# Block products for the second halves of the first two chunks of an attention-and-MLP kernel

## The chip, the cores and the metric

The kernel runs on one core of a Trainium2 chip. The core has a matrix engine (TensorE, PE in the profile), a vector engine (VectorE, DVE), a scalar engine (ScalarE, ACT), a general engine (GpSimd, POOL) and a sync engine (SyncE, SP) that issues most of the DMAs. The metric is the device time of one execution in microseconds (us).

## What is computed

Two blocks follow each other. The first is an attention whose feature map is a product of two small sketches; the second is an MLP with an exact GELU over all 4352 tokens:

```python
# q, k, v: (4 batches, 4 heads, 1088 tokens, 32); S1, S2: (8, 32)
def phi(x):
    a = np.einsum('rd,bhsd->bhsr', S1, x)
    b = np.einsum('rd,bhsd->bhsr', S2, x)
    return np.einsum('bhsi,bhsj->bhsij', a, b).reshape(*x.shape[:-1], 64)
q_p, k_p = phi(q), phi(k)
kv  = np.einsum('bhsf,bhsd->bhfd', k_p, v)
z   = np.sum(k_p, axis=2)
num = np.einsum('bhsf,bhfd->bhsd', q_p, kv)
den = np.einsum('bhsf,bhf->bhs', q_p, z)[..., None] + 1e-06
x   = (num / den).transpose(0, 2, 1, 3).reshape(4352, 128)
h   = x @ w_in                       # w_in (128, 2048)
g   = 0.5 * h * (1.0 + erf(h / sqrt(2)))
out = g @ w_out                      # w_out (2048, 128)
```

The weights arrive with 64 bits a number and are rounded to 32 bits on the chip.

## The kernel before

The tokens are worked in eight chunks of 512 (two for each batch) and a ninth of 256, which holds what is left of the four batches. For a chunk `n` the MLP runs over 16 inner tiles `fi` of 128 channels. A *step* is one pair `(n, fi)`. In a step TensorE makes the hidden product of the pair, ScalarE its GELU; the second half (the product with `w_out`) of an earlier pair, and pieces of attention for later chunks, are put into the same step.

The first hidden product and the GELU:

```python
def hidden(n, fi, by_halves=False):
    ps = hidden_bank()                              # one of two PSUM banks
    w = w_tile(w_in_sb, fi)
    for rows in (slice(0, 64), slice(64, 128)) if by_halves else (slice(0, 128),):
        pe.matmul(ps[rows, :W], lhsT=w[:, rows], rhs=xT[n][:, :W], start=True, stop=True)
    ...                                             # g_of[n, fi]: a tile "g", or a quarter of a "block"
    act.activation(out=g_of[n, fi][:, :W], in_=ps[:, :W], func=ACT.Gelu)
```

There are two ways for the second half. The usual one, for chunks 0, 1 and the last, adds 16 products in one PSUM bank:

```python
def project(n, fi, parts=range(B // 2)):
    first, final = fi == 0, fi == NF - 1
    if first:
        o_of[n] = out_bank() if n < NMAIN else [work_bank() for i in range(B // 2)]
    ...
    pe.matmul(o_of[n], lhsT=w_tile(w_out_sb, fi), rhs=g, start=first, stop=final)
```

The other, for chunks 2 to 7, splits pairs of tiles into 2x2 blocks and makes seven block products where there would be eight. Four sums of the weights are made once (`channel_sums`, GpSimd), four sums of the GELU's output for each block of four tiles (`token_sums`, GpSimd), and at the chunk's end the two PSUM banks are put together (`drain`, ScalarE and VectorE, and `combine`, VectorE):

```python
def token_sums(n, b):                               # after the GELU of tiles 4b to 4b + 3
    ...
    pool.tensor_sub(out=s[3], in0=a11, in1=a21)
    pool.tensor_add(out=s[1], in0=a21, in1=a22)
    pool.tensor_sub(out=s[2], in0=s[1], in1=a11)
    pool.tensor_sub(out=s[4], in0=a12, in1=s[2])

def two_products(n, b, i):                          # one of seven pairs of a block of four tiles
    ...
    if b == 0 and i == 0:
        acc[n] = [out_bank(), out_bank()]           # there are two out banks in all
    ...
        pe.matmul(acc[n][bank][half * 64:(half + 1) * 64, col:col + HW], lhsT=fixed, rhs=moving, ...)

def drain(n):
    act.copy(out=C[lo, 0], in_=a1[hi])
    act.copy(out=N[hi, 0, one], in_=a1[hi, one])
    act.copy(out=N[lo, 0, one], in_=a0[lo, one])
    dve.tensor_add(out=C[lo, 1], in0=a1[lo], in1=C[lo, 0])
    for half in (lo, hi):
        dve.tensor_add(out=C[half, 0, one], in0=a0[lo, one], in1=C[lo, 1, two])
    dve.tensor_add(out=C[hi, 0, two], in0=a0[hi, two], in1=C[hi, 0, one])
    dve.tensor_add(out=N[hi, 1, one], in0=a0[hi, one], in1=C[hi, 0, two])
    dve.tensor_add(out=N[lo, 1, one], in0=a0[lo, two], in1=N[lo, 0, one])
```

The order of the steps, and what is put into them (`at(step, what)`), for chunks 0 to 2:

```python
steps = [(n, fi) for f in range(0, NF, 4) for n in range(2) for fi in range(f, f + 4)]
steps += [(n, fi) for n in range(2, NCHUNK) for fi in range(NF)]
...
def round_at(t, w):                                 # from 64 bits to 32; takes a "bits_r" buffer, of which there are two
    at(t, lambda: (r.append(Rounding(w)), r[0].low_words(), r[0].fields()))
    at(t + 1, lambda: (r[0].exponents(), r[0].finish()))
for i, (t0, t1) in enumerate(((4, 6), (8, 10), (12, 20))):
    round_at(t0, w_in_sb[i + 2])
    round_at(t1, w_out_sb[i + 2])
for i in range(len(pieces)):
    at(22 + i, channel_sums, i)
b, t = 1, NCH * NF                                  # t = 32
at(t - 20, widen_v_rem, b)
for r in range(2):
    at(t - 18, key_turn_blocks, b, r)
for r in range(2):
    at(t - 17, features, b, r)
    at(t - 17, add_tokens, b, r, pool)              # writes k_s, in a "bits_r" buffer
at(t - 16, turn_keys_rem, b)
at(t - 15, features_rem, b)
at(t - 13, finish_keys, b)                          # TensorE reads k_s (L395); ScalarE copies kv_T
at(t - 12, lambda: turn_kv(1, held["kv"], by_act))
at(t - 13, query_turn, 2)
at(t - 11, query_expand, 2)
at(t - 8, attend, 2)
for n in range(3, NCHUNK):
    t = (n - 1) * NF
    at(t + 1 if n > 3 else t - 3, query_turn, n)    # VectorE, L452
    at(t + 2 if n > 3 else t - 2, query_expand, n)  # TensorE L461, ScalarE L468, VectorE L482
    ...
    at(t + 5, attend, n, ...)                       # TensorE L503, ScalarE L510, VectorE L511 and L515
```

`attend` ends in a chain: four copies on ScalarE, a reciprocal and four multiplies on VectorE, which make `xT[n]`. Within a step the text has this order: drains, the hidden product, token sums, the slots above, stores, second halves. Each engine works its instructions in the order of the text.

Of the kernel before, what the change touches and what calls it, by code (L numbers as in the profile page):

```python
# [16 lines left out]
def kernel(  # L17
# [33 lines left out]
    C = D + 1  # L51
    LAG = 2
    NMAIN = B * NCH
    FAST = 2
    NB = 4
    NCHUNK = NMAIN + 1
    assert B == 4 and d_model == 128 == H * D == JC * D == 2 * F and H == 4 and REM == 64 and NCH == 2

# [94 lines left out]

        return (a, 1) if a.dtype == FP else (a.bitcast(U32), 2)

    def load_w_in(i, gated=False):
        src, e = words(moe_w_in)
        c0, c1 = pieces[i]
        to = landing(w_in_sb[i], e == 2)
        if gated:  # L160

            pool.memset(to[0:1, 0:1], 0)
        sp.dma_start(out=to, in_=src[:, c0 * e:c1 * e])

    def load_w_out(i):
        src, e = words(moe_w_out)
        sp.dma_start(
            out=landing(w_out_sb[i], e == 2).rearrange("p (fo d) -> p fo d", d=d_model * e),
            in_=src[slice(*pieces[i]), :].rearrange("(fo fi) d -> fi fo d", fi=128))

    S_dst = landing(SR, S1.dtype != FP)
# [14 lines left out]
    load_q(1)  # L186
    load_w_in(1)
    load_w_out(0)
    load_w_out(1)

    def load_rest():

        for i in range(2, len(pieces)):
            load_w_in(i, gated=i == 2)
            load_w_out(i)
        for b in range(1, B):
            load_turned_k(b)
            load_main(sp, "v", b)
            for c in range(NCH):
                load_q(b * NCH + c)  # L200
            if b == 1:
                for n, b1 in (("k", 1), ("k", 3), ("v", 1), ("v", 2), ("v", 3)):
                    load_rem(n, b1)
        for b in range(B):
            load_rem("q", b)
# [224 lines left out]
        copy(out=kv_T[b], in_=ps[:, :128])  # L430

    def turn_kv(b, ps, copy):
        if b < 2:
            pe.transpose(ps[:, :128], in_=kv_T[b], identity=ident)
        else:
            for rows in (slice(0, 64), slice(64, 128)):
                pe.matmul(ps[rows, :128], lhsT=kv_T[b][:, rows], rhs=ident, start=True, stop=True)
        copy(out=kz[b].rearrange("p c n -> p (c n)"), in_=ps[:, :128])
# [119 lines left out]
    def hidden(n, fi, by_halves=False):  # L558
        W = width[n]
        ps = hidden_bank()  # L560
        w = w_tile(w_in_sb, fi)
        for rows in (slice(0, 64), slice(64, 128)) if by_halves else (slice(0, 128),):
            pe.matmul(ps[rows, :W], lhsT=w[:, rows], rhs=xT[n][:, :W], start=True, stop=True)  # L563
        if n < FAST:
            g_of[n, fi] = mlp.tile([128, CW], FP, name="g", bufs=4)
        else:
            if fi % NB == 0:
                blocks[n, fi // NB] = block(FP)
            g_of[n, fi] = blocks[n, fi // NB][:, fi % NB]
        act.activation(out=g_of[n, fi][:, :W], in_=ps[:, :W], func=ACT.Gelu)  # L570
# [40 lines left out]
    def factor(n, b, name, e):  # L611
# [9 lines left out]
        j = {"5": 1, "6": 2, "7": 3}[name[0]]  # L621
        return sums[n, b][j][:, e], T[j][:, k]

    def two_products(n, b, i):

        fours, ones_, sixes = [("4", "7", e, e) for e in range(2)], [("1", "5", e, e) for e in range(2)], ("6a", "6b", 0, 1)

        order = fours + ([sixes] + ones_ if b == 0 else ones_ + [sixes]) + [("2", "3", e, e) for e in range(2)]
        two = order[i]
        if b == 0 and i == 0:  # L630
            acc[n] = [out_bank(), out_bank()]
        for name, e in zip(two[:2], two[2:]):
            half, bank, col = PLACE[name]
            moving, fixed = factor(n, b, name, e)

            pe.matmul(acc[n][bank][half * 64:(half + 1) * 64, col:col + HW], lhsT=fixed, rhs=moving,  # L636
                      start=b == 0 and e == 0 and name in "4715", stop=b == NF // NB - 1, skip_group_check=True)

    drained = {}

    def drain(n):
# [15 lines left out]
        dve.tensor_add(out=N[lo, 1, one], in0=a0[lo, two], in1=N[lo, 0, one])  # L657
        drained[n] = C, N

    def combine(n):  # L660

        C, N = drained.pop(n)
        lo, hi, one, two = slice(0, 64), slice(64, 128), slice(0, HW), slice(HW, CW)
        dve.tensor_add(out=N[lo, 1, two], in0=C[lo, 1, one], in1=C[lo, 0, one])
        dve.tensor_add(out=N[hi, 1, two], in0=N[hi, 0, one], in1=C[hi, 0, two])
        return N[:, 1]

    def project(n, fi, parts=range(B // 2)):
        first, final = fi == 0, fi == NF - 1
        if first:  # L670
            o_of[n] = out_bank() if n < NMAIN else [work_bank() for i in range(B // 2)]
        g = g_of[n, fi]
        if n == NMAIN:

            for i in parts:
                pe.matmul(o_of[n][i][:, :128], lhsT=g[:, i * 128:(i + 1) * 128], rhs=w_tile(w_out_sb, fi),  # L676
                          start=first, stop=final)
            return
        pe.matmul(o_of[n], lhsT=w_tile(w_out_sb, fi), rhs=g, start=first, stop=final)  # L679

    def store(n):
        oT = mlp.tile([128, JC, d_model], FP, name="oT")
        if n == NMAIN:
            for i, (copy, eng) in enumerate(((by_dve, sp), (by_act, act))):
                copy(out=oT[:, i, :], in_=o_of[n][i][:, :128])
                for b, queue in ((i, eng), (i + 2, sp)):
                    queue.dma_start(out=out[b * S + MAIN:(b + 1) * S, :],
                                    in_=oT[b // 2 * REM:(b // 2 + 1) * REM, i, :])
            return

        dve.transpose(out=oT.rearrange("p n d -> p (n d)"), in_=o_of[n] if n < FAST else combine(n))
        row = n // NCH * S + n % NCH * CW
        if n < NCH:

            for c in range(d_model // 32):
                to = out[row:row + CW, c * 32:(c + 1) * 32].rearrange("(g t j) d -> j t g d", t=32, j=JC)
                o = oT[c * 32:(c + 1) * 32].rearrange("p n (m d) -> p (n m) d", d=32)
                o = o.rearrange("p (g j) d -> j p g d" if n == 0 else "p (j g) d -> j p g d", j=JC)
                for j in range(JC):
                    sp.dma_start(out=to[j], in_=o[j])  # L700
            return
        for c in range(d_model // 32):
            sp.dma_start(out=out[row:row + CW, c * 32:(c + 1) * 32].rearrange("(t n) d -> t n d", t=32),
                         in_=oT[c * 32:(c + 1) * 32].rearrange("p n (m d) -> p (n m) d", d=32))
# [74 lines left out]
        expand_multiply(1, i)  # L779


    steps = [(n, fi) for f in range(0, NF, 4) for n in range(2) for fi in range(f, f + 4)]
    steps += [(n, fi) for n in range(2, NCHUNK) for fi in range(NF)]
    slots = {t: [] for t in range(len(steps) + LAG)}

    def at(t, f, *a):
# [48 lines left out]
        at(t, lambda: (r.append(Rounding(w)), r[0].low_words(), r[0].fields()))  # L835
        at(t + 1, lambda: (r[0].exponents(), r[0].finish()))

    for i, (t0, t1) in enumerate(((4, 6), (8, 10), (12, 20))):
        round_at(t0, w_in_sb[i + 2])
        round_at(t1, w_out_sb[i + 2])  # L840
    for i in range(len(pieces)):
        at(22 + i, channel_sums, i)
    b, t = 1, NCH * NF
    at(t - 20, widen_v_rem, b)
    for r in range(2):
# [30 lines left out]
    done = {t: [] for t in range(len(steps) + LAG + 1)}  # L876
    drains = {t: [] for t in range(len(steps) + LAG + 1)}
    for t, (n, fi) in enumerate(steps):
        if n < FAST:
            products[t + LAG].append((project, n, fi))  # L880
            if fi == NF - 1:
                done[t + LAG + 1].append(n)
        elif n == NMAIN:
            at_ = max(t + LAG, (n * NF + 5) if fi < 3 else (n * NF + 6) if fi < 5 else 0)
            if fi < NF - 2:
                products[at_].append((project, n, fi))
            if fi == NF - 1:

                products[at_] += [(project, n, f, (i,)) for i in range(B // 2) for f in (fi - 1, fi)]
                done[at_ + 1].append(n)  # L890
        elif fi % NB == NB - 1:
            b = fi // NB
            for later, pairs in (((3, 3), (4, 2), (5, 2)) if b == 0 else ((2, 2), (3, 2), (4, 1), (5, 2))):
                for i in range(pairs):
                    products[t + later].append((two_products, n, b, len([p for q in products.values() for p in q
                                                                        if p[:3] == (two_products, n, b)])))
            if b == NF // NB - 1:
                drains[t + 6].append(n)
                done[t + 12].append(n)

    for t in range(len(steps) + LAG):
# [21 lines left out]
            drain(n)  # L923
        if t < len(steps):
            n, fi = steps[t]
            hidden(n, fi, by_halves=n >= FAST and (n < NMAIN or fi < 5))
        if t < len(steps) and FAST <= steps[t][0] < NMAIN and steps[t][1] % NB == NB - 1:
            token_sums(steps[t][0], steps[t][1] // NB)
        for f in slots[t]:
            f()  # L930
        for n in done[t]:
# [45 lines left out]
```

## Time and profile before

| | |
|---|---|
| time, median of 3 runs | 276.19 us (275.86 to 276.7) |
| span of the profiled execution | 274.7 us |
| TensorE busy | 268.2 us |
| VectorE busy | 157.7 us |
| ScalarE busy | 142.5 us |
| GpSimd busy | 146.9 us |
| HBM read, written | 10.90 MB, 2.23 MB |

In the profile, a row of a group names the line of the kernel (L563 is the hidden product, L679 the usual second half, L636 a block product), the engine, the operation, what it writes and reads, its shape and count, then busy time and mean duration. The chain that ended last is followed back from the last instruction and printed in order of time: start in us, duration in us, engine, tile, line. A waiting engine shows "<-" and what released it.

### The profile page before, as it was taken

What the parts mean: (1) busy time and instruction counts of PE and PEld (TensorE: products, weight loads), DVE (VectorE), ACT (ScalarE), POOL (GpSimd) and SP (SyncE); (2) the same over time, 40 slices, a digit from 0 to 9 for tenths busy, and PEclk for the clock granted to TensorE, in tenths of its full rate; (3) what the DMA queues carried; (4) which work ended last, traced back from release to release, by engine and by line L of the source; (5) the groups of instructions that cost most, each with busy time, mean ns of one, the idle gap of its engine ahead of it and who ended that gap; (6) DMA issues with size and microseconds to landing.
All of it is one profiled execution on the core that took longest, in us unless ns stands there. A gap on an engine that the chain in (4) does not pass through costs nothing.

```text
span 274.7 us, 5546 instructions
## 1 busy us (share of the span) xinstructions
PE 268.2 (98%) x2215; PEld 135.5 (49%) x2215; DVE 157.7 (57%) x248; ACT 142.5 (52%) x283; POOL 146.9 (53%) x158
## 2 busy tenths in 40 slices
PE   8989999999999999999999999999999999999993
PEld 6745444543432545435545445344444444455793
DVE  6986788434953398179407799488037902750230
ACT  4684764366454633583357533673367334733441
POOL 3331001942003699558875699468866876777300
PEclk9999999999999999999999999999999999999999
DMA  6669273626101210000200000200200020010020
GB/s 207 194 185 306 52 167 68 173 68 166 19 0 22 34 24 2 2 0 1 41 1 2 0 2 2 38 0 2 38 0 2 0 41 0 2 26 15 4 38 19
DMA packets 37914, 13.49 MB, mean 49 GB/s; under 512 B 28288, under 2 KB 37248, under 8 KB 37888
## 3 DMA queue, kind: packets, MB, share of 16 engines
q1 hardware_dynamic: 37728, 13.08, 19.3%
q8 instruction: 17, 0.28, 0.4%
q14 instruction: 9, 0.07, 0.1%
q10 hardware_dynamic: 160, 0.05, 0.1%
HBM read 10.90 MB, written 2.23 MB: 48 GB/s over the span
## 4 chain that ended last, share of the span: by engine, by line
PE 96%; DMA 1%; DVE 1%; issue 0%; ACTq 0%; ACT 0%; DVEq 0%
PE h_ps L563 43%; PE o_ps L636 27%; PE o_ps L679 11%; PE w_ps L461 3%; PE w_ps L676 3%; PE w_ps L503 2%; PE w_ps L395 1%; PE w_ps L349 1%; DMA raw_SR<-in_S_dram 1%; PE o_ps L404 1%; PE h_ps L529 0%; PE w_ps L424 0%; PE w_ps L529 0%; PE o_ps L305 0%; PE o_ps L709 0%
## 5 line engine op out<-in xcount | busy, mean ns | idle before, releaser
L563 PE MATMUL h_ps<-xT,w_in 128*64 128x512 f32 (+3 forms) x490 | 140.6, 576 | 0.2 <-DVE xT L548 0.2
L570 ACT ACTIVATE block<-h_ps 128x512 f32<-128x512 f32 (+1 forms) x112 | 63.2, 567 | 86.2 <-PE h_ps L563 83.1
L563 PEld LDWEIGHTS h_ps<-xT,w_in 128*64 128x64 f32 (+1 forms) x490 | 43.3, 146 | 35.7 <-issue 15.5
L605 POOL TENSOR_TENSOR bits_low<-block 128x512 f32<-128x512 f32 x24 | 31.5, 1312 | 50.5 <-ACT block L570 50.4
L636 PE MATMUL o_ps<-block,w_out 128*64 128x256 f32 x192 | 49.5, 380 | 0.0
L482 DVE TENSOR_TENSOR q_pT<-A_sb,w_ps 64x512 f32<-64x512 f32 x32 | 22.1, 691 | 35.9 <-ACT A_sb L468 35.3
L636 PEld LDWEIGHTS o_ps<-block,w_out 128*64 128x64 f32 x192 | 25.7, 137 | 32.4 <-issue 24.8
L606 POOL TENSOR_TENSOR bits_a<-block 128x512 f32<-128x512 f32 x24 | 31.0, 1291 | 12.3 <-ACT block L570 12.2
L679 PE MATMUL o_ps<-g,w_out 128*128 128x512 f32 x64 | 33.5, 607 | 0.1
L607 POOL TENSOR_TENSOR bits_e<-bits_a,block 128x512 f32<-128x512 f32 x24 | 31.3, 1305 | 1.9
L608 POOL TENSOR_TENSOR bits_m<-block,bits_e 128x512 f32<-128x512 f32 x24 | 30.9, 1286 | 1.9
L511 DVE RECIPROCAL den<-den 128x512 f32<-128x512 f32 (+1 forms) x7 | 21.9, 3122 | 15.6 <-ACT den L510 15.6
L570 ACT ACTIVATE g<-h_ps 128x512 f32<-128x512 f32 x32 | 19.1, 597 | 21.0 <-PE h_ps L563 20.9
L636 PE MATMUL o_ps<-bits_a,small 128*64 128x256 f32 x96 | 24.9, 382 | 0.0
L636 PE MATMUL o_ps<-bits_m,w_out 128*64 128x256 f32 x96 | 24.6, 379 | 0.0
L636 PE MATMUL o_ps<-bits_low,small 128*64 128x256 f32 x96 | 24.6, 379 | 0.0
L636 PE MATMUL o_ps<-block,small 128*64 128x256 f32 x96 | 24.6, 379 | 0.0
L636 PEld LDWEIGHTS o_ps<-block,small 128*64 128x64 f32 x96 | 13.1, 137 | 15.6 <-issue 11.4
L468 ACT COPY A_sb<-w_ps 64x512 f32<-64x512 f32 (+1 forms) x36 | 17.6, 557 | 3.8 <-PE w_ps L461 3.7
L515 DVE TENSOR_TENSOR xT<-w_ps,den 32x512 f32<-32x512 f32 (+1 forms) x28 | 18.2, 649 | 1.0
L679 PEld LDWEIGHTS o_ps<-g,w_out 128*128 128x128 f32 x64 | 11.2, 189 | 14.3 <-issue 14.1
L510 ACT ACTIVATE den<-w_ps 32x512 f32<-32x512 f32 (+1 forms) x28 | 15.6, 558 | 1.4 <-PE w_ps L503 1.1
(161 smaller groups left out, 302.8 us busy)
## 6 DMA issues: line engine op xcount, KB each, us to landing
block<-in_moe_w_in_dram SPq DMA_DIRECT2D x3, 512.0 KB, 6.4
block<-in_moe_w_out_dram SPq DMA_DIRECT2D x3, 512.0 KB, 10.3
k<-in_k_dram SPq DMA_DIRECT2D x48, 32.0 KB, 1.9
v<-in_v_dram SPq DMA_DIRECT2D x3, 512.0 KB, 4.8
q<-in_q_dram SPq DMA_DIRECT2D x24, 64.0 KB, 3.7
out_dram<-oT SPq DMA_DIRECT2D x24, 64.0 KB, 2.2
k<-in_k_dram SPq DMA_DIRECT2D x2, 256.0 KB, 2.9
q<-in_q_dram SPq DMA_DIRECT2D x2, 256.0 KB, 4.8
```

Of the source, the lines that this page charges most:

```text
L468: act.copy(out=A[g // 2][F:, g % 2, :width[n]], in_=B_of[n][g // 2][:F, g % 2, :width[n]])
L482: dve.tensor_mul(out=cols[r * F:(r + 1) * F], in0=a[:, :, r::2], in1=b[:, :, r::2])
L511: dve.reciprocal(out=den[:, :W], in_=den[:, :W])
L515: dve.tensor_mul(out=xT[n][rows, :W], in0=banks[h % 2][rows, :W], in1=den[rows, :W])
L563: pe.matmul(ps[rows, :W], lhsT=w[:, rows], rhs=xT[n][:, :W], start=True, stop=True)
L570: act.activation(out=g_of[n, fi][:, :W], in_=ps[:, :W], func=ACT.Gelu)
L605: pool.tensor_sub(out=s[3], in0=a11, in1=a21)
L606: pool.tensor_add(out=s[1], in0=a21, in1=a22)
L607: pool.tensor_sub(out=s[2], in0=s[1], in1=a11)
L608: pool.tensor_sub(out=s[4], in0=a12, in1=s[2])
L636: pe.matmul(acc[n][bank][half * 64:(half + 1) * 64, col:col + HW], lhsT=fixed, rhs=moving, start=b == 0 and e == 0 and name in "4715", sto ...
L679: pe.matmul(o_of[n], lhsT=w_tile(w_out_sb, fi), rhs=g, start=first, stop=final)
```

## The change

For chunks 0 and 1 only the first eight inner tiles keep the usual second half; their sum is copied aside by ScalarE (`take_usual`). The other eight tiles go by block products, chunk 0's eight steps first and then chunk 1's, where before the two chunks took turns of four steps to the end. `combine` adds the copy. Hidden products are made as two halves from step 18 on (before, from chunk 2 on, step 32), so that they have the form of the block products. The rounding of the last piece of `w_out` and two of the channel sums come earlier, since they are needed earlier. The second piece of `w_out` is loaded with the later pieces, behind a gate. In the ninth chunk more products are left to the end, ordered so that the first of the two output banks is complete sooner; both are copied by VectorE, and the four last stores go on two queues, two each. The purpose is less TensorE work and a shorter end.

```diff
+    USUAL = 8
@@ loads
     load_w_out(0)
-    load_w_out(1)
     def load_rest():
+        load_w_out(1, gated=True)
         for i in range(2, len(pieces)):
-            load_w_in(i, gated=i == 2)
+            load_w_in(i)
             load_w_out(i)
@@ turn_kv
-        if b < 2:
+        if b == 0:
             pe.transpose(ps[:, :128], in_=kv_T[b], identity=ident)
@@ two_products
+    def first_block(n):
+        return USUAL // NB if n < NCH else 0
@@
+    def take_usual(n):
+        usual[n] = mlp.tile([128, CW], FP, name="g", bufs=4)
+        act.copy(out=usual[n], in_=o_of[n])
@@ combine
+        if n in usual:
+            dve.tensor_add(out=N[:, 1], in0=N[:, 1], in1=usual[n])
@@ store of the ninth chunk
-            for i, (copy, eng) in enumerate(((by_dve, sp), (by_act, act))):
-                copy(out=oT[:, i, :], in_=o_of[n][i][:, :128])
-                for b, queue in ((i, eng), (i + 2, sp)):
+            for i in range(B // 2):
+                dve.tensor_copy(out=oT[:, i, :], in_=o_of[n][i][:, :128])
+                for b, queue in ((i, sp), (i + 2, act)):
@@ steps
-    steps = [(n, fi) for f in range(0, NF, 4) for n in range(2) for fi in range(f, f + 4)]
-    steps += [(n, fi) for n in range(2, NCHUNK) for fi in range(NF)]
+    steps = [(n, fi) for f in range(0, USUAL, 4) for n in range(NCH) for fi in range(f, f + 4)]
+    steps += [(n, fi) for n in range(NCHUNK) for fi in range(USUAL if n < NCH else 0, NF)]
@@ rounding and channel sums
-    for i, (t0, t1) in enumerate(((4, 6), (8, 10), (12, 20))):
+    for i, (t0, t1) in enumerate(((4, 6), (8, 10), (12, 17))):
         round_at(t0, w_in_sb[i + 2])
         round_at(t1, w_out_sb[i + 2])
-    for i in range(len(pieces)):
-        at(22 + i, channel_sums, i)
+    for i, t in enumerate((25, 26, 28, 13, 19)):
+        at(t, channel_sums, i)
@@ second halves (drains[t + 6] as for the other chunks)
-        if n < FAST:
+        if n < NCH and fi < USUAL:
             products[t + LAG].append((project, n, fi))
-            if fi == NF - 1:
-                done[t + LAG + 1].append(n)
+            if fi == USUAL - 1:
+                slots[t + LAG + 1].append(lambda n=n: take_usual(n))
@@ ninth chunk
-            if fi < NF - 2:
+            if fi < NF - 4:
                 products[at_].append((project, n, fi))
             if fi == NF - 1:
-                products[at_] += [(project, n, f, (i,)) for i in range(B // 2) for f in (fi - 1, fi)]
+                products[at_] += [(project, n, NF - f, (i,)) for f, i in ((4, 0), (3, 0), (2, 0), (4, 1), (1, 0), (3, 1),
+                                                                          (2, 1), (1, 1))]
@@ each step
-            hidden(n, fi, by_halves=n >= FAST and (n < NMAIN or fi < 5))
+            hidden(n, fi, by_halves=t >= 18 and (n < NMAIN or fi < 5))
```

(Cut: the hidden products of the new block tiles go into a `block`, and the token sums are made for the new blocks too.)

More of the change, by code (lines that the diff above doesn't have):

```diff
@@ L53 @@
     NMAIN = B * NCH
-    FAST = 2
     NB = 4
+    USUAL = 8
     NCHUNK = NMAIN + 1
@@ L154, in words, with load_w_in, load_w_out @@
         return (a, 1) if a.dtype == FP else (a.bitcast(U32), 2)
-    def load_w_in(i, gated=False):
+    def load_w_in(i):
         src, e = words(moe_w_in)
         c0, c1 = pieces[i]
-        to = landing(w_in_sb[i], e == 2)
+        sp.dma_start(out=landing(w_in_sb[i], e == 2), in_=src[:, c0 * e:c1 * e])
+    def load_w_out(i, gated=False):
+        src, e = words(moe_w_out)
+        to = landing(w_out_sb[i], e == 2)
         if gated:
             pool.memset(to[0:1, 0:1], 0)
-        sp.dma_start(out=to, in_=src[:, c0 * e:c1 * e])
-    def load_w_out(i):
-        src, e = words(moe_w_out)
         sp.dma_start(
-            out=landing(w_out_sb[i], e == 2).rearrange("p (fo d) -> p fo d", d=d_model * e),
+            out=to.rearrange("p (fo d) -> p fo d", d=d_model * e),
             in_=src[slice(*pieces[i]), :].rearrange("(fo fi) d -> fi fo d", fi=128))
@@ L622, in factor @@
         return sums[n, b][j][:, e], T[j][:, k]
+    def first_block(n):
+        return USUAL // NB if n < NCH else 0
     def two_products(n, b, i):
         fours, ones_, sixes = [("4", "7", e, e) for e in range(2)], [("1", "5", e, e) for e in range(2)], ("6a", "6b", 0, 1)
-        order = fours + ([sixes] + ones_ if b == 0 else ones_ + [sixes]) + [("2", "3", e, e) for e in range(2)]
+        opens = b == first_block(n)
+        order = fours + ([sixes] + ones_ if opens else ones_ + [sixes]) + [("2", "3", e, e) for e in range(2)]
         two = order[i]
-        if b == 0 and i == 0:
+        if opens and i == 0:
             acc[n] = [out_bank(), out_bank()]
@@ L636, in two_products @@
             pe.matmul(acc[n][bank][half * 64:(half + 1) * 64, col:col + HW], lhsT=fixed, rhs=moving,
-                      start=b == 0 and e == 0 and name in "4715", stop=b == NF // NB - 1, skip_group_check=True)
+                      start=opens and e == 0 and name in "4715", stop=b == NF // NB - 1, skip_group_check=True)
     drained = {}
@@ L658, in drain @@
         drained[n] = C, N
+    usual = {}
+    def take_usual(n):
+        usual[n] = mlp.tile([128, CW], FP, name="g", bufs=4)
+        act.copy(out=usual[n], in_=o_of[n])
     def combine(n):
@@ L665, in combine @@
         dve.tensor_add(out=N[hi, 1, two], in0=N[hi, 0, one], in1=C[hi, 0, two])
+        if n in usual:
+            dve.tensor_add(out=N[:, 1], in0=N[:, 1], in1=usual[n])
         return N[:, 1]
     def project(n, fi, parts=range(B // 2)):
-        first, final = fi == 0, fi == NF - 1
+        first, final = fi == 0, fi == (USUAL if n < NCH else NF) - 1
         if first:
@@ L689, in store @@
             return
-        dve.transpose(out=oT.rearrange("p n d -> p (n d)"), in_=o_of[n] if n < FAST else combine(n))
+        dve.transpose(out=oT.rearrange("p n d -> p (n d)"), in_=combine(n))
         row = n // NCH * S + n % NCH * CW
@@ L878 @@
     for t, (n, fi) in enumerate(steps):
-        if n < FAST:
+        if n < NCH and fi < USUAL:
             products[t + LAG].append((project, n, fi))
-            if fi == NF - 1:
-                done[t + LAG + 1].append(n)
+            if fi == USUAL - 1:
+                slots[t + LAG + 1].append(lambda n=n: take_usual(n))
         elif n == NMAIN:
             at_ = max(t + LAG, (n * NF + 5) if fi < 3 else (n * NF + 6) if fi < 5 else 0)
-            if fi < NF - 2:
+            if fi < NF - 4:
                 products[at_].append((project, n, fi))
             if fi == NF - 1:
-                products[at_] += [(project, n, f, (i,)) for i in range(B // 2) for f in (fi - 1, fi)]
+                products[at_] += [(project, n, NF - f, (i,)) for f, i in ((4, 0), (3, 0), (2, 0), (4, 1), (1, 0), (3, 1),
+                                                                          (2, 1), (1, 1))]
                 done[at_ + 1].append(n)
@@ L892 @@
             b = fi // NB
-            for later, pairs in (((3, 3), (4, 2), (5, 2)) if b == 0 else ((2, 2), (3, 2), (4, 1), (5, 2))):
+            for later, pairs in (((3, 3), (4, 2), (5, 2)) if b == first_block(n) else ((2, 2), (3, 2), (4, 1), (5, 2))):
                 for i in range(pairs):
@@ L925 @@
             n, fi = steps[t]
-            hidden(n, fi, by_halves=n >= FAST and (n < NMAIN or fi < 5))
-        if t < len(steps) and FAST <= steps[t][0] < NMAIN and steps[t][1] % NB == NB - 1:
-            token_sums(steps[t][0], steps[t][1] // NB)
+            hidden(n, fi, by_halves=t >= 18 and (n < NMAIN or fi < 5))
+        if t < len(steps) and steps[t][0] < NMAIN and steps[t][1] % NB == NB - 1:
+            n, b = steps[t][0], steps[t][1] // NB
+            if b >= first_block(n):
+                token_sums(n, b)
         for f in slots[t]:
```

## The prediction

> **What bounds the kernel now.** I read the page's busy times first, then the groups kept apart by shape, then the chain that ended last, and last the order of time on VectorE and on the queues.
>
> ```profile
> PE 268.2 (98%) x2215; PEld 135.5 (49%) x2215; DVE 157.7 (57%) x248; ACT 142.5 (52%) x283; POOL 146.9 (53%) x158
> PEclk9999999999999999999999999999999999999999
> PE 96%; DMA 1%; DVE 1%; issue 0%; ACTq 0%; ACT 0%; DVEq 0%
> ```
>
> TensorE is busy 98% of the span at a full clock, and the chain that ended last runs on it for 96%. So any TensorE time removed is gained and any TensorE wait made is lost, one for one; nobody else is near full on average.
>
> ```profile
> L679 PE MATMUL o_ps<-g,w_out 128*128 128x512 f32 x64 | 33.5, 607 | 0.1
> L636 PE MATMUL o_ps<-block,w_out 128*64 128x256 f32 x192 | 49.5, 380 | 0.0
> ```
>
> L679 is the usual second half, L636 the block products. Their mean durations overlap each other, so I price from the chain, which shows the pace (start, us, what; the stage from step 24 to step 38):
>
> ```profile
> 65.48 1.02 PE w_ps L503 x8
> 66.50 1.06 PE o_ps L679 x2
> 67.55 0.86 PE h_ps L563 x2
> ...
> 76.99 1.07 PE w_ps L461 x8
> ...
> 82.90 1.01 PE h_ps L563 x4
> 83.91 1.06 PE o_ps L679 x2
> 84.97 3.64 PE h_ps L563 x16
> ...
> 90.53 1.01 PE h_ps L563 x4
> ```
>
> A 128x512 matmul (two records, or four as halves) is 0.86 us; four records of L636 are 0.43 (the chain's steady "x8" is 0.86). A change of form costs extra: a full-width matmul after another form 1.06 instead of 0.86 (+0.20), a half-width one 1.01 (+0.15). There is no wait in this stage. L503 at 65.48 is the attention product of chunk 2 (step 24), L461 at 76.99 the query product of chunk 3 (step 30), L563 at 90.53 the hidden product of step 38.
>
> VectorE in the same stretch (start, us, engine, line, what):
>
> ```profile
> 68.98 3.35 DVE L511 RECIPROCAL den<-den 128x512 f32<-128x512 f32 x1 [4.30 <-ACT den L510]
> 72.44 2.79 DVE L515 TENSOR_TENSOR xT<-w_ps,den 32x512 f32<-32x512 f32 x4
> 75.26 0.71 DVE L452 STREAM_TRANSPOSE qT<-q 128x512 f32<-128x512 f32 x1
> ```
>
> Behind the attention product stands a serial chain: ScalarE's four copies, the reciprocal, four multiplies, and only then the turn of chunk 3's queries that L461 needs. It ends at 75.97; L461 starts at 76.99. VectorE is 57% busy, yet here it is one microsecond from holding TensorE up.
>
> The end of the kernel:
>
> ```profile
> 270.44 1.87 SPq L687 DMA_DIRECT2D out_dram<-oT  x3
> ```
>
> Three stores are issued one after another on one queue, 0.62 us each, the last one from 271.68 to 272.31.
>
> **What the Trainium skill says.** (1) "TensorE: Matmul & The Clock Gate", table at its head: VectorE, ScalarE and GpSimd work their queue in strict order. The trace agrees: qT at 75.26 needs nothing from xT and still starts only when xT is done. (2) "DMA: Bandwidth & Descriptors", section "Issuing engines are not separate DMA queues": issuing from two engines saves only the time to initiate. That is what the tail has to save; the row above shows it as 0.62 us a store. (3) "Perfetto Trace Analysis", section "Tensor Engine Instruction (MATMUL, LD_WEIGHTS)": reported ends are modelled. The trace agrees, 607 ns a record at a pace of 430, hence the chain and not busy time.
>
> **The change, part by part.**
>
> *Seven products for eight.* For four inner tiles the usual way costs 4 x 0.86 = 3.44 us, the block products 7 x 0.43 = 3.01. There are two such groups in each of two chunks: 4 x 0.43 = 1.72 us off TensorE.
>
> *One form throughout.* From step 18 hidden products are halves, and no full-width product follows until the end. Before, the path from step 18 (51.10) to step 38 has nine form changes, seven at 0.20 and two at 0.15, 1.7 us (five of them between 80.84 and 84.97). After, I count some six at 0.15 (after the sums of keys, each query product, the attention product, and at step 18): 0.9. Saved: 0.8. Together TensorE has 2.4 us less to do, rounding the two.
>
> *A wait on ScalarE at steps 18 to 20.* Rounding of the last w_out piece moves from step 20 to 17. It writes a bits_r buffer; there are two, and both then hold the key sums of batch 1, which TensorE reads in step 19 (L395, 1.25 us). Step 18 starts at 51.10: halves 1.01, hidden of step 19 0.86, key sums to 54.2. Only then may ScalarE do the exponents (0.71), the copy of the usual half (0.57), the delayed GELU (0.60) and the kv copy (0.27): 56.5. TensorE has meanwhile done the rest of the sums (0.39) and step 20's hidden (1.01), to 55.6, and waits for that copy to turn kv: about 1.0 us lost. The stretch from step 18 to the attention product of step 24 comes to 12.7 us (before 65.48 - 51.10 = 14.4).
>
> *A wait on VectorE at step 30.* This is the largest doubtful term. Chunk 0's drain now falls in step 29, ahead of the turn of chunk 3's queries in the text. Its six adds, by the rows of the later drains (0.68, and five near 0.42), are 2.8 us. Before, L461 could start 75.97 - 65.48 = 10.5 us after the attention product; now 10.5 + 2.8 = 13.3, some 13.4 with the signal. TensorE arrives sooner: 1.02 attention, 1.01 twos, then steps 25 to 29 and hidden 30 at 1.72 + 1.72 + 1.29 + 1.72 + 0.86 + 0.86 = 10.2. It waits 3.2 us.
>
> *From L461 to step 38:* 1.07, three pairs 1.44, steps 31 to 34 at 1.72, steps 35 and 36 at 1.29 and 1.72, then 0.86 + 1.02 + 0.90: 15.2 us (before 13.5). The chunk 1 drain in step 37 lies where later chunks have theirs, without a TensorE wait.
>
> *Sum of the middle:* 12.7 + 13.4 + 15.2 = 41.3 against 39.4, so +1.8: 2.4 saved, 4.2 waited.
>
> *The sums on GpSimd.* Four tensors of 1.28 us for each block, 5.1, against a TensorE pace of 6.4. Worked through, the third sum is needed about a microsecond after it is there at step 22, more elsewhere; the channel sums (four of 0.46) go between. Hidden, I think.
>
> *Loads.* The second w_out piece waits to about 15.1 and, first in the queue, should land by 20 (its peers took about 5.4 us at most); VectorE first touches it at 21.80. Zero on the path, perhaps 0.1 at the head.
>
> *The end.* TensorE's last product ends near 270.55; with VectorE's copy (the same in the old trace, 0.29) the last store is issued near 270.9, on both queues at once, instead of 271.68: -0.75 us. TensorE does the same work in another order.
>
> Total: 276.19 + 1.8 - 0.75 = 277.2.
>
> **Rivals.** *A: the query turn isn't held up* (VectorE gets the drain done inside gaps, or TensorE is late at step 24 to 29 anyhow, which uses up the same wait). For it: the author placed the pieces step by step, and 3 us would be seen. Against it: the three VectorE rows above are packed with no gap that a 2.8 us drain could use. It gives 277.2 - 3.2 = 274.0. *B: neither wait appears*: 273.0; the buffer count speaks against. *C: GpSimd becomes the bound* in steps 19 to 36, since sums, channel sums and key sums meet there: two late blocks of about one us give 279. The 53% average speaks against, the slice at 50 to 60 us (nearly full) for it. *D: the loads start later and hold up the rounding*: under 1 us, as they are used 5 us and more after landing.
>
> **Range and chances.** The sum is 277.2; I give the waits about two chances in three and rival A one in four, and shade to 276.9. The low end 273.4 covers A and most of B, the high end 278.5 one more late engine. Two per cent is 5.5 us, more than any of these: faster 0.02, same 0.95, slower 0.03.
>
> **What would show it.** In the changed profile: TensorE busy share falling from 98% to about 96%; waits of TensorE for VectorE's qT before a L461 near 74 us, about 3 us long, and for ScalarE's kv_T near 56 us, about 1 us; L679 records 32 instead of 64; an exponent step of ScalarE released by L395; the last store's issue under 271 us relative to the old end of TensorE work. If TensorE shows no wait between 50 and 92 us, my two waits are wrong and the time is near 273. If it waits for bits_low or bits_e, rival C is right.

## The result and the profile after

The changed kernel takes 280.06 us (median of four runs, 278.9 to 280.65) against 276.12 for the kernel before: the ratio, estimated from the single executions, is 1.0135 (the medians alone give 1.0143), with a 95% interval of 1.0096 to 1.0173. The prediction was 276.9 us, 273.4 to 278.5, and its sum 277.2. The change makes the kernel slower by more than the prediction's range has room for.

The changed kernel's busy times, the granted clock (the share of its full clock that TensorE got) in 40 slices of the span, and the chain by engine:

```profile
PE 267.4 (96%) x2326; PEld 136.9 (49%) x2326; DVE 172.5 (62%) x267; ACT 145.6 (53%) x290; POOL 167.5 (60%) x174
PEclk9999999999979999999999999999999999999999
PE 83%; DVE 10%; ACT 3%; DMA 1%; issue 1%; POOL 0%; SPq 0%; DVEq 0%; ACTq 0%; POOLq 0%
```

TensorE's share falls from 98 to 96%, VectorE and GpSimd gain 15 and 21 us of work, the chain leaves TensorE for VectorE for a tenth of the span, and one slice, the twelfth, has a clock under full. TensorE's waits by engine and line (us in total, times, longest):

```profile
PE w_ps L462 <- DVE qT L453: 3.7, 2, 3.2
PE w_ps L722 <- DVE idle L229: 1.2, 1, 1.2
PE w_ps L438 <- ACT kv_T L431: 0.8, 1, 0.8
PE h_ps L564 <- ACT xT L549: 0.2, 1, 0.2
```

The L722 and L564 rows stand in the profile of before too, there as L709 and L563. New are the two waits of the prediction, 0.8 us for kv_T and 3.2 us for qT, and a second, smaller one for qT (3.7 less 3.2: 0.5 us, ahead of chunk 4's query product at 116.67 us). The two of the prediction, the wait in brackets:

```profile
55.59 0.44 PE L438 MATMUL w_ps<-ident,kv_T 128*64 128x128 f32 x4 [0.76 <-ACT kv_T L431]
76.27 2.09 PE L462 MATMUL w_ps<-qT,Srep 32*128 32x512 f32 x8 [3.23 <-DVE qT L453]
```

The chain around the long wait (start, us, what):

```profile
71.33 0.88 PE h_ps L564 x4
...
72.62 0.69 DVE sums L657
...
75.19 0.42 DVE sums L662
75.60 0.63 DVE qT L453
76.23 0.04 issue
76.27 2.09 PE w_ps L462 x8
78.36 2.01 PE o_ps L641 x12
80.38 0.86 PE h_ps L564 x4
```

L657 to L662 are the drain of chunk 0, ahead of the query turn L453 (VectorE's transpose of chunk 3's queries into qT), as the prediction had it. What it did not have is in the last three rows: L462 takes 2.09 us where it took 1.07 before, and the twelve records after it 2.01 where three pairs should take 1.44. The same stretch microsecond by microsecond (first the view's heading):

```profile
core 0: us, PE busy (x) PEld busy (x) DVE busy (x) ACT busy (x) POOL busy (x), PEclk, DMA share, GB/s
75.00:76.00 1.00, 0.00 (x0) 0.00 (x0) 0.99 (x3) 0.00 (x0) 0.92 (x3) 1.00 0.00 0
76.00:77.00 1.00, 0.73 (x4) 0.52 (x8) 0.22 (x1) 0.00 (x0) 1.00 (x2) 0.53 0.00 0
77.00:78.00 1.00, 1.00 (x8) 0.00 (x0) 0.00 (x0) 0.00 (x0) 0.27 (x1) 0.50 0.00 0
78.00:79.00 1.00, 1.00 (x8) 0.52 (x6) 0.00 (x0) 0.56 (x2) 0.00 (x0) 0.50 0.00 0
79.00:80.00 1.00, 1.00 (x10) 0.54 (x10) 0.47 (x1) 1.00 (x4) 0.00 (x0) 0.76 0.00 0
```

TensorE comes back from 3.2 us without work and runs at half clock for some 3.4 us.

Where the 2.4 us between the two spans (274.7 and 277.1) arise, from the starts of the same instructions in both chains:

| stage | before | after | difference | predicted |
|---|---|---|---|---|
| start to the first hidden product | 17.91 | 17.27 | -0.64 | 0, perhaps 0.1 |
| from there to step 18 | 33.19 | 33.19 | 0 | 0 |
| step 18 to the attention product of step 24 | 14.38 | 12.38 | -2.0 | -1.7 |
| from there to L462 of step 30 | 11.51 | 13.43 | +1.9 | +1.9 |
| from there to step 38 | 13.54 | 16.83 | +3.3 | +1.7 |
| from there to TensorE's end | 180.0 | 180.5 | +0.5 | 0 |
| TensorE's end to the span's end | 4.2 | 3.5 | -0.6 | -0.75 |

The first row is not the change: in traces of the variants below, the first hidden product starts anywhere from 17.05 to 18.19 us.

### The profile page after: what moved, and what is told of

It reads as the page before. It is cut to its first block, busy times and chain, and to the rows that moved or that the text cites. A ratio compares the mean times of both kernels' runs of the same rounds, so it can differ in the third digit from the quotient of the medians.

```text
span 277.1 us, 5815 instructions
## 1 busy us (share of the span) xinstructions
PE 267.4 (96%) x2326; PEld 136.9 (49%) x2326; DVE 172.5 (62%) x267; ACT 145.6 (53%) x290; POOL 167.5 (60%) x174
## 4 chain that ended last, share of the span: by engine, by line
PE 83%; DVE 10%; ACT 3%; DMA 1%; issue 1%; POOL 0%; SPq 0%; DVEq 0%; ACTq 0%; POOLq 0%
PE h_ps L564 38%; PE o_ps L641 28%; PE o_ps L692 5%; PE w_ps L462 3%; PE w_ps L689 3%; PE w_ps L504 2%; DMA k<-in_k_dram 1%; DVE den L512 1%; DVE bits_r L388 1%; PE w_ps L350 1%; DVE bits_r L391 1%; DVE q_pT L483 1%; PE w_ps L396 1%; ACT den L511 1%; DVE xT L516 1%
## 5 line engine op out<-in xcount | busy, mean ns | idle before, releaser
L564 PE MATMUL h_ps<-xT,w_in 128*64 128x512 f32 (+3 forms) x518 | 140.7, 577 | 0.2 <-ACT xT L549 0.2
L571 ACT ACTIVATE block<-h_ps 128x512 f32<-128x512 f32 (+1 forms) x128 | 72.8, 570 | 93.6 <-PE h_ps L564 89.5
L641 PE MATMUL o_ps<-block,w_out 128*64 128x256 f32 x224 | 57.8, 380 | 0.0
L564 PEld LDWEIGHTS h_ps<-xT,w_in 128*64 128x64 f32 (+1 forms) x518 | 42.2, 143 | 29.6 <-issue 10.1
L606 POOL TENSOR_TENSOR bits_low<-block 128x512 f32<-128x512 f32 x28 | 36.5, 1305 | 30.9 <-ACT block L571 30.7
L607 POOL TENSOR_TENSOR bits_a<-block 128x512 f32<-128x512 f32 x28 | 36.3, 1296 | 20.0 <-ACT block L571 19.9
L608 POOL TENSOR_TENSOR bits_e<-bits_a,block 128x512 f32<-128x512 f32 x28 | 36.5, 1302 | 2.2
L609 POOL TENSOR_TENSOR bits_m<-block,bits_e 128x512 f32<-128x512 f32 x28 | 36.1, 1288 | 2.2
L641 PE MATMUL o_ps<-bits_low,small 128*64 128x256 f32 x112 | 29.4, 386 | 0.0
L657 DVE TENSOR_TENSOR sums<-o_ps,sums 64x512 f32<-64x512 f32 x8 | 5.5, 682 | 24.1 <-ACT sums L654 20.7
L641 PE MATMUL o_ps<-bits_e,small 128*64 128x256 f32 x112 | 16.9, 379 | 0.0
L692 PE MATMUL o_ps<-g,w_out 128*128 128x512 f32 x32 | 16.5, 603 | 0.1
```

## The experiments

**The changed kernel again.**

> The changed kernel once more, to see what of its 280.06 us repeats. Theory 1 (two waits of TensorE, 0.8 us for kv_T and 3.2 us for qT, and 1.7 us of half clock behind the longer one): both waits and the half clock are there again at the same places, the span is 277 to 279 us. Theory 2 (the profiled run, 278.9, was the quick one of four for a reason that its trace doesn't show, and the usual run has one more wait): the new trace has a further wait of 1 us or more somewhere.

279.68 us (278.51 to 280.86), ratio 1.0131 [1.0103, 1.0158]. Both waits are there (0.77 and 3.24 us), and so is the half clock. It begins later here, at about 78 us, a microsecond after the work came back at full clock, and lasts beyond 81. There is no further wait of a microsecond; theory 1 holds.

The clock is not lost every time. Over a whole execution its mean is 0.994 in all four executions of the result and in five of the six here, and 1.000 in the sixth, which is also the quickest (278.51 us).

**The drain behind the query turn.** In step 29 chunk 0's drain moves behind what is put into the step:

```diff
-                drains[t + 6].append(n)
+                if n == 0:
+                    slots[t + 6].append(lambda: drain(0))
+                else:
+                    drains[t + 6].append(n)
```

> Chunk 0's drain stands behind the turn of chunk 3's queries in step 29 instead of ahead of it, all else as changed. Theory 1 (the drain's six adds on VectorE, 2.8 us, hold up qT and so L462): the 3.2 us wait shrinks to 0.3 to 0.5 us, the half clock behind it goes too, and the time falls by 4 to 5 us, to about 275.5. Rival (the turn is late because of the reciprocal and the four multiplies of chunk 2 alone, the drain is hidden): the wait stays above 2 us and the time falls by under 1 us. Rival (taking the drain away from there makes the block products of step 30 wait for its banks instead): the wait moves to L641, the time falls by under 2 us.

275.86 us (274.66 to 277.27), ratio 0.9986 [0.9974, 0.9998]. The wait at L462 of step 30 is 0.35 us, the clock full throughout, and the block products wait for no bank:

```profile
74.45 1.14 PE L462 MATMUL w_ps<-qT,Srep 32*128 32x512 f32 x8 [0.35 <-DVE qT L453]
PEclk9999999999999999999999999999999999999999
```

Against the repeat, six VectorE adds in the wrong place cost 3.8 us of time, though they last 2.8 us. Both rivals fall.

**A filler in the wait.** TensorE gets products of zeros to do while it waits; the wait for qT is not shortened:

```diff
     def query_expand(n):
+        if n == 3:
+            keep_busy(6, work_bank())
         expand_products(n)
```

> Six matrix products of zeros (128x128 by 128x256, some 0.43 us each, 2.6 us in all, into a free bank) are put on TensorE ahead of chunk 3's query product, where it waits 3.2 us; all else as changed. Theory 1 (the half clock from 76 to 79.5 us comes of the idle time itself): the clock stays at 1.00, L462 takes 1.07 instead of 2.09 us and the time falls by 1.5 to 1.9 us though the wait is not shortened. Rival (the clock falls for another reason at this place, or a fixed time after the start): no change, within 0.5 us. If the spread of the changed kernel's runs (278.9 to 280.65) comes of the clock, it shrinks here to under 0.8 us.

278.43 us (277.93 to 279.13), ratio 1.0079 [1.0063, 1.0096]: 1.25 us less than the repeat of the changed kernel, 1.6 less than its first four runs. TensorE, with the filler (L724) in the wait:

```profile
73.93 2.86 PE L724 MATMUL w_ps<-idle 128*128 128x256 f32 x12
77.24 1.14 PE L462 MATMUL w_ps<-qT,Srep 32*128 32x512 f32 x8 [0.45 <-DVE qT L453]
```

L462 takes 1.14 us, as in the run above, and the clock is full. So the half clock comes of the idle time: extra work of no use makes the kernel faster. The gain is a little below the expected 1.5 if the repeat is the yardstick; it is what the repeat's one execution at full clock gains on its median too, 1.2 us. The spread, 1.2 us, did not shrink to under 0.8; it has some other source as well.

**A third bits_r buffer.** Room comes from one buffer fewer each of `bits_high` and `a_rem`:

```diff
-... name=f"bits_{x}", bufs=2 if x == "r" else 3)
+... name=f"bits_{x}", bufs=3)
-        words = mlp.tile([128, LC], U32, name="bits_r")
+        words = mlp.tile([128, LC], U32, name="bits_r", bufs=3)
```

> A third bits_r buffer, so that the rounding of the last w_out piece does not wait for the key sums; room for it comes from one buffer fewer each for two small tiles used early. All else as changed. Theory 1 (the 0.8 us wait for kv_T comes of the shared buffer): ScalarE's exponents no longer wait for L396, the wait of L438 for kv_T falls under 0.2 us and the time falls by 0.6 to 0.9 us; the 3.2 us wait stays, since its chain starts with the attention product. Rival (ScalarE is late from its load in steps 18 to 20, not from the wait): the wait for kv_T stays above 0.5 us and the time within 0.3 us.

279.92 us (278.08 to 280.93), ratio 1.0125 [1.0096, 1.0155]. The wait for kv_T is gone, so its cause is settled. The time isn't shorter, against the theory: this trace has two other waits on VectorE, 0.84 us for kT (the transposed keys) and 0.49 us for chunk 2's qT at 57.69. (The clock again: 0.994 in four of the six executions, 0.985 in one, 1.000 in the quickest, 278.08 us.)

```profile
45.62 1.32 PE L350 MATMUL w_ps<-S,kT 64*64 64x32 f32 x64 [0.84 <-DVE kT L335]
```

VectorE ahead of the first one:

```profile
42.62 1.64 DVE L275 SCALAR_TENSOR_TENSOR bits_e<-block,bits_r 128x512 uint32<-128x512 uint32 x1 [0.54 <-ACT bits_r L262]
44.29 0.83 DVE L280 TENSOR_TENSOR w_in<-bits_m,bits_e 128x512 f32<-128x512 f32 x1
45.04 1.41 DVE L335 STREAM_TRANSPOSE kT<-k 128x256 f32<-128x256 f32 x4
```

and GpSimd at that time, which makes the channel sums that the change moved to step 13:

```profile
42.06 0.40 POOL L326 COPY v_rem_aug<-v_rem 64x64 f32<-64x64 f32 x2 [17.61 <-DMA v_rem<-in_v_dram]
42.43 0.45 POOL L593 TENSOR_TENSOR small<-w_out 128x128 f32<-128x128 f32 x1
42.84 0.45 POOL L594 TENSOR_TENSOR small<-w_out 128x128 f32<-128x128 f32 x1
43.25 0.45 POOL L595 TENSOR_TENSOR small<-w_out,small 128x128 f32<-128x128 f32 x1
43.78 0.78 POOL L596 TENSOR_TENSOR small<-w_out,small 128x128 f32<-128x128 f32 x1
```

L275 takes 0.69 us in the profiled run of the changed kernel, where GpSimd comes to these sums only after it, because the load of v_rem landed later:

```profile
42.39 0.69 DVE L275 SCALAR_TENSOR_TENSOR bits_e<-block,bits_r 128x512 uint32<-128x512 uint32 x1 [0.54 <-ACT bits_r L262]
43.18 0.90 POOL L326 COPY v_rem_aug<-v_rem 64x64 f32<-64x64 f32 x2 [18.95 <-DMA v_rem<-in_v_dram]
44.04 0.45 POOL L593 TENSOR_TENSOR small<-w_out 128x128 f32<-128x128 f32 x1
```

The Trainium skill, "SBUF — State Buffer", section "Who interferes with whom", says that a VectorE instruction with two SBUF inputs and a GpSimd instruction that reads SBUF exclude each other. The traces agree: L275 has two such inputs and more than doubles, while the drain's adds, with one input in PSUM, keep 0.42 us beside a GpSimd busy throughout (74.28 to 75.61 in the changed kernel).

**The channel sums later**, on top of the drain behind the turn:

```diff
-    for i, t in enumerate((25, 26, 28, 13, 19)):
+    for i, t in enumerate((25, 26, 28, 16, 19)):
```

> As the run with the drain behind the turn (275.86 us), and the channel sums of the fourth w_out piece in step 16 instead of 13, so that GpSimd makes them after the key sums and not beside VectorE's rounding ahead of the turn of the keys. Theory (GpSimd beside VectorE stretches VectorE's operations on SBUF, 0.69 to 1.6 us, and in some runs that delays kT and L350 by 0.9 us): L350 never waits for kT, VectorE's L275 and L280 near 42 to 45 us keep 0.69 us, the spread falls from 2.6 to under 2 us and the median by 0.2 to 0.5 us. Rival (the spread comes of the first 18 us alone): no change of the median within 0.15 us, same spread.

276.51 us, ratio 1.0004 [0.9991, 1.0016]; 275.87 to 277.19 but for one execution of 280.33, which is left out of the ratio, as is one each of 279.23, 277.39 and 276.65 in three of the sets below. L275 and L280 keep 0.7 us in this trace, L350 does not wait, and the spread is 1.3 us, as expected:

```profile
42.74 0.70 DVE L275 SCALAR_TENSOR_TENSOR bits_e<-block,bits_r 128x512 uint32<-128x512 uint32 x1 [0.54 <-ACT bits_r L262]
43.47 0.69 DVE L280 TENSOR_TENSOR w_in<-bits_m,bits_e 128x512 f32<-128x512 f32 x1
```

But the time did not fall. The channel sums now come ahead of the first token sums (L606, L607) and push these onto the rounding of w_out, where L280 takes 1.67 us; chunk 2's turn stands behind it, and L462 waits 1.07 us:

```profile
54.10 1.27 POOL L606 TENSOR_TENSOR bits_low<-block 128x512 f32<-128x512 f32 x1
55.80 1.27 POOL L607 TENSOR_TENSOR bits_a<-block 128x512 f32<-128x512 f32 x1 [0.43 <-ACT block L571]
55.95 1.67 DVE L280 TENSOR_TENSOR w_out<-bits_m,bits_e 128x512 f32<-128x512 f32 x1
58.30 1.14 PE L462 MATMUL w_ps<-qT,Srep 32*128 32x512 f32 x8 [1.07 <-DVE qT L453]
```

The collision was moved, not removed. The expected gain is a miss.

**The end of before**, on top of the drain behind the turn: stores, copies and product order of the ninth chunk undone.

> As the run with the drain behind the turn (275.86 us), with the end of the kernel before: three last stores on one queue, the second bank copied by ScalarE, the last products in the old order. Theory (the end is shorter by the serial issue of stores): from the end of TensorE's work to the end of the span 4.1 us instead of 3.5, the time rises by 0.5 to 0.8 us. Rival (the landing sets the end, not the issue): no change within 0.2 us.

276.33 us (275.32 to 277.86), ratio 1.0002 [0.9985, 1.002]. From TensorE's end to the end of the span it is 4.1 us instead of 3.5, as the theory says; the time rises by 0.47 us by the medians, a little under the expected 0.5, and the two intervals overlap.

**The load of before**, on top of the drain behind the turn: the second piece of w_out ungated, in its old place, and the gate back on the third piece of w_in.

> As the run with the drain behind the turn (275.86 us), with the second piece of w_out loaded in its old place, without its gate. Theory (the later load does nothing for the path): the first hidden product starts within the range of the other traces (17.05 to 18.19 us) and the time is the same within 0.3 us. Rival (it clears the way for earlier loads): the first hidden product starts at 17.9 us or later and the time rises by 0.4 us or more.

276.02 us (274.96 to 276.88), ratio 0.9987 [0.9976, 0.9997]: the same time. The first hidden product starts at 17.24 us without the late load and between 17.05 and 18.19 with it. No effect of the later load shows.

**All waits taken away.** Third bits_r buffer, channel sums in step 16, and the turns ahead of VectorE's long chains:

```diff
-        at(t + 1 if n > 3 else t - 3, query_turn, n)
+        at({3: 23, 4: 36}.get(n, t + 1), query_turn, n)
```

> The changed kernel with its waits taken away: the turn of chunk 3's queries in step 23 and of chunk 4's in step 36, ahead of the long chains of VectorE; a third bits_r buffer; the channel sums of the fourth piece in step 16. Theory (all that the block products save is there once these waits go: 2.4 us less work and 0.6 us at the end): TensorE waits for nothing over 0.3 us after the first hidden product, the time is 273 to 274 us, 0.8 to 1.1% under the kernel before. Rival (each wait taken away is followed by the next one on VectorE, as with the third buffer alone): 275 us or more.

273.33 us (273.21 to 273.37), ratio 0.9883 [0.987, 0.9897]: faster than the kernel before, by 1.2%. TensorE's waits in full, and its clock:

```profile
PE w_ps L722 <- DVE idle L229: 1.2, 1, 1.2
PE h_ps L564 <- ACT xT L549: 0.2, 1, 0.2
PEclk9999999999999999999999999999999999999999
```

All of the change's waits are gone, and the time is 3.1 us under that of before in the same set of runs (276.41). The chain shows where. Steps 18 and 38 begin here:

```profile
51.31 1.87 PE h_ps L564 x8
88.11 1.01 PE h_ps L564 x4
```

From the one to the other it is 36.8 us, before 39.4, so 2.6 less; and from TensorE's end to the end of the span it is 3.55 us, before 4.2, so 0.6 less.

Four variants of this one each put one part back:

**Channel sums at step 13.**

> As the run with the turns ahead (273.33 us), with the channel sums of the fourth piece back in step 13. Theory (GpSimd beside VectorE's rounding delays kT in some runs by 0.9 us): the time is 0.1 to 0.9 us longer and its spread over 0.5 us; where the trace has VectorE's L275 at 1.6 us, L350 waits for kT. Rival (the place of these sums makes no difference once VectorE has the turns ahead): 273.3, within 0.15 us.

273.88 us, ratio 0.9919 [0.9907, 0.9932], 272.97 to 275.45. In its trace L275 takes 2.01 us and L350 waits 1.21 us for kT. The theory holds: 0.55 us in the median, and a spread of 2.5 us where the five executions with the sums in step 16 lie within 0.16.

**Two bits_r buffers.**

> As the run with the turns ahead (273.33 us), with two bits_r buffers as in the changed kernel. Theory (the shared buffer costs TensorE a wait for kv_T, which shows in the time once nothing behind it on VectorE takes it up): a wait of 0.8 us for kv_T, and of up to 1 us for qT in step 21, the time 0.8 to 1.3 us longer. Rival (it is taken up later, as with the third buffer in the changed kernel): within 0.2 us.

275.06 us (274.77 to 275.65), ratio 0.9963 [0.9949, 0.9976]: 1.7 us more. TensorE waits 0.77 us for kv_T and then 1.07 us for chunk 2's qT, whose turn stands behind the delayed and stretched rounding on VectorE (L280 1.67 us). That is more than expected. It is the wait of the run with the channel sums later, and it takes both: the traces with two buffers and the sums in step 13, and the one with three buffers and the sums in step 16, have no such wait.

**The end of before.**

> As the run with the turns ahead (273.33 us), with the end of the kernel before (three last stores on one queue, old order of the last products). Theory: 0.4 to 0.8 us longer, 273.8 to 274.1. Rival: within 0.2 us.

273.67 us (272.91 to 274.2), ratio 0.9908 [0.9891, 0.9926]: 0.34 us more by the medians, not clear of the intervals; in the trace 4.1 us instead of 3.55 after TensorE's end.

**The load of before.**

> As the run with the turns ahead (273.33 us), with the second piece of w_out loaded in its old place. Theory (the later load does nothing): within 0.2 us. Rival (it clears the way for the earlier loads): 0.3 us longer or more.

272.86 us, ratio 0.9883 [0.9867, 0.9899]. The medians stand 0.47 us apart, the shorter without the later load, and the intervals overlap: nothing gained by it.

## Why the prediction was wrong

*Saved work: right.* 2.4 us was predicted, though its two parts, 1.72 and 0.8, add up to 2.5. With all waits away the trace shows 2.6 us, and 3.1 us is measured for this and the end together.

*The wait on ScalarE, "about 1.0 us lost": right in mechanism and near in size.* 0.8 us by the trace, and the third buffer removes it. The prediction's own durations add up to 56.35, not 56.5, which gives 0.7. But it ended the effect there; VectorE stands behind the same buffer, and in the kernel with the sums in step 16 that adds 1.07 us.

*The wait on VectorE at step 30, "It waits 3.2 us": right.* 3.23 us, and the stretch from the attention product 13.43 us for 13.4. Rival A, which the shading to 276.9 leaned on, is refuted by this trace. The shading cost 0.3 us.

*"any TensorE wait made is lost, one for one": this step failed.* The wait of 3.2 us cost more than its length, because TensorE lost its clock after it: 1.02 us in L462 (2.09 - 1.07) and 0.57 in the products behind it (2.01 - 1.44; with all waits away they take 1.45), 1.6 us, the whole excess of the fifth row of the table. The filler run shows that the idle time is the cause. The prediction saw "PEclk" full in all 40 slices and has no term for the clock; but in the kernel before, no wait of TensorE is longer than 1.2 us. The Trainium skill has this: "TensorE: Matmul & The Clock Gate", Part 1, section "What's actually happening", gives half clock after an idle window of about 3.4 us and a return after a busy one. The traces agree in the half rate and in its length; for the idle time the measurement decides, and 3.2 us was enough in all three traces with this wait, and by the mean clock in 14 of the 16 executions with it.

*"The chunk 1 drain in step 37 lies where later chunks have theirs, without a TensorE wait": right for the drain, wrong for what follows.* The store of chunk 1, six steps on, adds three VectorE operations on SBUF beside GpSimd. In the kernel before, chunk 4's turn came straight behind the last of the key sums (L390 ended and L452 began at 108.2 us); in the changed kernel the store stands between the two:

```profile
110.66 1.50 DVE L675 TENSOR_TENSOR sums<-sums 64x256 f32<-64x256 f32 x1
112.17 1.41 DVE L676 TENSOR_TENSOR sums<-sums 64x256 f32<-64x256 f32 x1
113.62 1.66 DVE L678 TENSOR_TENSOR sums<-sums,g 128x512 f32<-128x512 f32 x1
115.31 0.71 DVE L704 STREAM_TRANSPOSE oT<-sums 128x512 f32<-128x512 f32 x1
115.94 0.67 DVE L453 STREAM_TRANSPOSE qT<-q 128x512 f32<-128x512 f32 x1
```

L675 and L676 take 0.41 and 0.42 us at their shortest and L678 0.69; here 4.6 us for 1.5. Chunk 4's turn stands behind them, and L462 waits 0.5 us. With the turn moved to step 36 the store takes as long, and nothing waits.

*The sums on GpSimd, "Hidden, I think": only half right.* No TensorE row waits for them, so rival C falls. But beside VectorE they stretch its operations, which makes kT late in some runs (0.84 to 1.21 us, in three of the eight traces that have the fourth piece's sums in step 13; neither trace of the changed kernel as it stands is among them).

*The end, -0.75: right in direction, 0.5 to 0.6 us by the traces, though the times alone (0.47 and 0.34 us) do not show it clear of noise. The load, zero: no effect shows.*

In sum: 277.2, less 0.3 for the stage from step 18 to step 24 (-2.0 for -1.7), and 1.6 for the clock, 0.5 for chunk 4's turn, 0.15 for the end, make about 279.2. What lies between this and 279.7 or 280.06 is not settled. Late kT is a candidate, as the spread with and without the sums in step 13 says; so are the first 18 us: the changed kernel's two traces differ by 0.8 us in span, and 0.5 us of it is there at the first hidden product (17.27 and 17.75).

## What to carry to other kernels

Where one engine is full, work saved on it counts only if what the change gives to the others is placed ahead of nothing that this engine waits for: go through each engine's order of text, not its share of busy time. A wait of three microseconds on TensorE can cost more than its length: here it took the clock as well, for another 1.6 us, in most executions. Where the order can't be changed, useless products in the gap can win back the second part.

## What the runs showed of the hardware

- After 3.2 us without work TensorE's clock was granted at 0.50 for some 3.4 us, in three of three traces; two of the 16 executions with this wait kept a mean clock of 1.000. In one trace the half clock came with the first product, in the repeat about 1 us later: it is not tied to the instruction.
- A VectorE operation with both inputs in SBUF beside GpSimd operations on SBUF took 1.41 to 2.01 us for 0.42 to 0.69 at its shortest; the drain's adds, with one input in PSUM, kept 0.42. L256, whose one input is in SBUF, took 1.50 for 0.42 beside GpSimd's key sums.
- Which engine pays depends on the exact times. Where v_rem landed early enough for GpSimd's channel sums of step 13 to lie beside L275, L275 took 1.64 to 2.01 us in three traces; in a fourth, with the load of before, it kept 0.73 and two of GpSimd's sums took 0.95 and 0.90 us for 0.45.
